# Token stores moved from ScalarE's queue to SyncE's, and extra weight for streaming heads in the pacing of attention

## The chip, the cores and the metric

The kernel runs on one core of one Trainium2 chip. The metric is the device time of an execution in microseconds (us), as the median over several executions. Six fast runs of the kernel before, on the same chip, spread by 1.0% (392.65 to 396.69 us). Runs come with a state. Only runs of the state "fast" enter a ratio; a single run of one core has the state "unknown". The granted clock is the share of its full clock that TensorE got. PSUM is where the kernel puts the products of its matmuls (pA, pV and pO in the traces), in tiles that are called banks here. Engines: PE is TensorE (PEld its weight loads), ACT is ScalarE, DVE is VectorE, POOL is GpSimd, SP is SyncE. A line of a timeline gives start and length in us, the engine and the line of the kernel, the operation, what it writes <- reads, shapes and count, and in brackets how long the engine had been idle and what ended that. The lines shown are word for word; those between them are left out.

## The reference

The program is an attention followed by a mixture of four expert networks:

```python
# attention: q, k, v of shape (4 batches, 8 heads, 768, 64)
scores = scale * q @ k.T                       # causal
# heads 0, 2, 6 ("retrieval") see every earlier key
# heads 1, 3, 4, 5, 7 ("streaming") see 4 sink keys and a window of 64
a = softmax(scores);  x = (a @ v)              # to rows: 3072 tokens x 512
# experts: E = 4, hidden 1024
p = domain_probs / domain_probs.sum(-1)
out = sum_e p[:, e] * (relu(x @ w1[e]) @ w2[e])  # 3072 x 512, float32
```

## The kernel before

The 768 positions of a batch are two chunks of 384 tokens, so attention has chunks 0 to 7. The expert networks run over 24 tiles of 128 tokens: tiles 0 to 2 together and tile 3 alone in a plain way (`plain_steps`), then ten pairs of tiles in a way with fewer products (`pair_steps`). Attention of a later chunk is put out in small steps between the matmuls of the experts; the order is fixed when the program is built.

The stores of the first four tiles, in `plain_steps`:

```python
            else:
                nc.vector.scalar_tensor_tensor(out=acc[nt], in0=ps_o, ...)   # L1002
            if e == E - 1:
                nc.scalar.dma_start(out=out[nt * P : (nt + 1) * P, :], in_=acc[nt])  # L1008
            yield FTP // 2 * mm_ns(DM), 1.4
```

The end of a streaming head (Ln and then Exp of its negative give one over the row's sum; `ps` is one of two pV banks of PSUM; `later` puts the scaling out some 1300 planned ns after this):

```python
            nc.scalar.activation(out=rc[r, :], in_=ps[o, 0:CH], func=AF.Ln, ...)   # L769
            ...
                nc.scalar.activation(out=rc[r, :], ..., func=AF.Exp, scale=-1.0)   # L779
                later(scale, g)            # L774: xT = ps * rc, which frees the bank
            ...
            yield ns + (600.0 if g == 1 else 0.0)     # planned ns of this step
```

The pacing. Each step of the experts yields its matmul time and a share; each step of attention its planned ns:

```python
    def att_ns(a):                       # planned ns of chunk a
        ns = 4000.0 if a % NCH == 0 else 6100.0
        return ns + (1100.0 + HP * 3 * 400.0 + NSH * 600.0 if a < NCH else 0.0)
    ...
    for ns, share in moe_steps():
        spent += ns * share
        while state["a"] < G and spent > plan[state["a"]][0]:
            lo, hi = plan[state["a"]]
            behind_plan = (spent - lo) / (hi - lo) * att_ns(state["a"])
            if state["steps"] is not None and state["done"] >= behind_plan:
                break
            attention_step()
```

`share` is 0.5 in the first layer of a pair, where ScalarE does the ReLUs, and 1.57 in the products of its second layer, where ScalarE has little to do: by the page of before, 94.6 us of ReLUs (L1087) against 11.2 us of copies (L1129).

The softmax here doesn't subtract the row's maximum and nothing guards it: scores larger than these inputs give would overflow.

Of the kernel before, what the change touches and what calls it, by code (L numbers as in the profile page):

```python
# [17 lines left out]
def kernel(  # L18
# [33 lines left out]
    nc = tc.nc  # L52
    P = 128
# [3 lines left out]
    NCH = S // CH  # L57
    N = B * S
    HP = H // 2
# [39 lines left out]
    def bank():  # L99
        return pA.tile([P, 512], FP32, name="pA", bufs=4)  # L100
# [4 lines left out]
    NR, NSH = len(RH), len(SH)  # L105
# [49 lines left out]
    def half(u):  # L155
        return slice(u * D, (u + 1) * D)
# [25 lines left out]
    def v_tile(b, c, h, t):  # L182

        if b:
            return v_tiles(b, c, h)[:, t, :]
        return v_tiles(b, t // TC, h)[:, t % TC, :]
# [188 lines left out]
    for h in range(H):  # L375
        if h == 2:
            nc.sync.dma_start(
                out=v_s32, in_=v[0, :, 0:NS, :].rearrange("h r d -> r h d")
# [16 lines left out]
        out=probs, in_=moe_domain_probs.rearrange("(t p) e -> p t e", p=P)  # L395
# [14 lines left out]
    def warm_up(ps, n, cols):  # L410
        for _ in range(n):
            nc.tensor.matmul(
                out=ps[:, 0:cols], lhsT=warm[:, 0:P], rhs=warm[:, 0:cols],
                start=True, stop=True,
            )
# [101 lines left out]
    def mm_ns(cols):  # L517
        return cols / 2.4 + 2.5

    def attention(b, c):  # L520
        g = b * NCH + c
# [212 lines left out]
        def values(h):  # L734
            if RETR[h]:
                yield from values_r(h)
                return
            ct, u = PLACE[h]
            if first and u == 1:
                ps = pO.tile([P, 512], FP32, name="pO", bufs=2)  # L740
            else:
                ps = pV.tile([P, 512], FP32, name="pV", bufs=2)
            if first:
                warm_up(ps, {3: 4, 4: 4, 5: 6, 7: 10}.get(h, 0), 256)
            work = []
            for es, parts in es_of[h]:
                for t, o, q0, nq in parts:
                    work.append((es, t, o, q0, nq))
            ns = 0
            for n, (es, t, o, q0, nq) in enumerate(work):  # L750
                nc.tensor.matmul(  # L751
                    out=ps[:, q0 : q0 + nq],
                    lhsT=v_tile(b, c, h, t),
                    rhs=es[:, o : o + nq],
                    start=(n == 0),
                    stop=(n == len(work) - 1),
                    skip_group_check=True,
                )
                ns += mm_ns(nq)
                if ns > 300 and n < len(work) - 1:  # L760
                    yield ns
                    ns = 0

            r, o = half(u), half(1 - u)
            pair = first and h in (3, 4)
            if not pair or u == 0:
                rc_of[0] = att.tile([P, CH], FP32, name="rc", bufs=2)
            rc = rc_of[0]
            nc.scalar.activation(  # L769
                out=rc[r, :], in_=ps[o, 0:CH], func=AF.Ln, bias=eps[o, :]  # L770
            )

            def scale(r=r, ps=ps):
                nc.vector.tensor_tensor(  # L774
                    out=xT[g][r, ct, :], in0=ps[r, 0:CH], in1=rc[r, :], op=ALU.mult
                )

            if not pair:
                nc.scalar.activation(out=rc[r, :], in_=rc[r, :], func=AF.Exp, scale=-1.0)  # L779
                later(scale, g)  # L780
            elif u == 0:
                scale_of[0] = scale
            else:
                nc.scalar.activation(out=rc, in_=rc, func=AF.Exp, scale=-1.0)
                later(scale_of[0], g)
                later(scale, g)

            yield ns + (600.0 if g == 1 else 0.0)

        def both(a, bb):  # L790

# [11 lines left out]
        if first:  # L803
# [8 lines left out]
            sink_row(5)  # L812
            sink_row(7)
            yield from both(scores(1), values(0))
            yield from transposes(2)
            yield from both(scores(3), values(2))
            x_transposes(0)
            yield from scores(4)
            yield from transposes(3)
            yield from values(1)  # L820
            yield from both(scores(5), values(3))
            yield from both(scores(6), values(4))
# [87 lines left out]
    def later(op, g):  # L910
        behind.append((clock[0] + LAG, op, g))
# [34 lines left out]
    acc = {}  # L946

    def acc_of(nt):
        n0 = 2 * FTP * CH + nt * 2 * DM if nt < 3 else 6 * KT * P - 2 * DM
        return hA[:, n0 : n0 + 2 * DM].bitcast(FP32)  # L950

    def plain_steps(nt0, tiles, e, tokens, n0):

        cols_n = tiles * P
        hs = hA[:, n0 : n0 + FTP * cols_n].rearrange("p (f x) -> p f x", f=FTP)
        require(nt0 // 3)
        x = tokens()
        ahead = 4 if nt0 == 0 and e == 0 else 1
        for f0 in [0, *range(ahead, FTP)]:
            pss = {ft: bank() for ft in range(f0, f0 + (1 if f0 else ahead))}  # L960
            cts = (0, 2, 1, 3)

            def layer1(ft, n):
                ct = cts[n]
                nc.tensor.matmul(  # L965
                    out=pss[ft][:, 0:cols_n],
                    lhsT=w1sb[:, e * DMP + ct, ft * P : (ft + 1) * P],
                    rhs=x[:, ct, :],
                    start=(n == 0),
                    stop=(n == DMP - 1),  # L970
                )

            for ft in pss:
                for n in range(DMP - 1):
                    layer1(ft, n)
            for ft, ps in pss.items():
                layer1(ft, DMP - 1)
                nc.scalar.activation(  # L978
                    out=hs[:, ft, :], in_=ps[:, 0:cols_n], func=AF.Relu
                )  # L980
                yield DMP * mm_ns(cols_n), 0.6
        for j in range(tiles):
            nt = nt0 + j
            ps_o = pO.tile([P, DM], FP32, name="pO", bufs=2)
            for ft in range(FTP):
                nc.tensor.matmul(  # L986
                    out=ps_o,
                    lhsT=hs[:, ft, j * P : (j + 1) * P],
                    rhs=w2sb[:, e * FTP + ft, :],
                    start=(ft == 0),  # L990
                    stop=(ft == FTP - 1),
                )
                if ft == FTP // 2 - 1:
                    yield FTP // 2 * mm_ns(DM), 1.4
            p_ap = p_sb[:, nt, e : e + 1]
            if e == 0:
                acc[nt] = acc_of(nt)
                nc.vector.tensor_scalar(
                    out=acc[nt], in0=ps_o, scalar1=p_ap, scalar2=None, op0=ALU.mult
                )  # L1000
            else:
                nc.vector.scalar_tensor_tensor(  # L1002
                    out=acc[nt], in0=ps_o, scalar=p_ap, in1=acc[nt],
                    op0=ALU.mult, op1=ALU.add,
                )
            if e == E - 1:

                nc.scalar.dma_start(out=out[nt * P : (nt + 1) * P, :], in_=acc[nt])  # L1008
            yield FTP // 2 * mm_ns(DM), 1.4

    PT = 2
# [207 lines left out]

    def att_ns(a):  # L1220
        ns = 4000.0 if a % NCH == 0 else 6100.0
        return ns + (1100.0 + HP * 3 * 400.0 + NSH * 600.0 if a < NCH else 0.0)

    first_pair = E * UNIT + ONE

# [26 lines left out]
    def require(a):  # L1252
        drained = False
        while state["a"] <= a:
            attention_step()
            drained = True
        if drained:
            tick(LAG)
        while any(g <= a for _, _, g in behind):
            behind.pop(0)[1]()  # L1260

    spent = 0.0
    for ns, share in moe_steps():
        spent += ns * share
        tick(ns)
# [6 lines that stand above are left out]
# [37 lines left out]
```

## Time and profile before

| | before |
|---|---|
| median of 4 runs | 396.42 us (395.07 to 397.28) |
| span of the profiled run | 392.6 us |
| TensorE busy | 376.8 us, 96% |
| longest single wait of TensorE | 3.52 us, at 76.9 us |
| late excess (after 84 us) | 4.85 us in eight places |

"Late excess" is used throughout: the distance from each matmul's start to the next, less columns / 2.4 + 2.5 ns, summed where it is over 0.15 us and the clock is full. The formula fits the trace of before: after 84 us the median distance is 56, 109, 163 and 216 ns for 128, 256, 384 and 512 columns, and the formula gives 55.8, 109.2, 162.5 and 215.8. The late excess is worked out from the starts in the trace and shows losses that busy time hides, because the ends of matmuls are modelled. The page's line on the chain that ended last says how much of the span hung on TensorE itself:

```profile
PE 75%; DMA 15%; POOL 4%; ACT 3%; issue 1%; DVE 1%; SPq 1%; ACTq 0%; POOLq 0%
```

A quarter of the chain ran through something else. The other lines of before stand in the prediction.

### The profile page before, as it was taken

To read this page: it belongs to the slowest core of one execution; us is meant where nothing else is said; L and a number is where in the kernel's file an instruction comes from. 1 tells how busy PE (TensorE), PEld (TensorE's weight loads), DVE (VectorE), ACT (ScalarE), POOL (GpSimd) and SP (SyncE) were. 2 spreads that over 40 slices of the span, in tenths; PEclk is the share of its full clock that TensorE was granted. 3 is DMA by queue.
4 is the path that set the end of the run, shared out by engine and by line. 5 is a ranking of instruction groups with operands and counts; after the bars stand their busy time and mean duration, and the time that the engine had idled before them with its cause. 6 is when DMAs were issued, how large, how long until landed. Compare 5 with 4: busy or idle time off the path is not lost.

```text
span 392.6 us, 9368 instructions
## 1 busy us (share of the span) xinstructions
PE 376.8 (96%) x3814; PEld 312.7 (80%) x3814; DVE 231.4 (59%) x516; ACT 234.4 (60%) x476; POOL 110.4 (28%) x152
## 2 busy tenths in 40 slices
PE   7989999889999997999999999999999999999996
PEld 4755456457897886889988898889988898888885
DVE  7736787516957657575654656575654556454440
ACT  3853569335767767574865667574865667450640
POOL 8834553582028206601550006601300000000000
PEclk9999999989999999999999999999999999999999
DMA  8999999999199968936890448924910210110101
GB/s 158 161 209 199 177 152 192 175 189 103 55 114 96 114 131 67 165 80 89 102 149 4 109 94 64 162 79 84 107 54 2 69 55 12 55 54 21 38 0 55
DMA packets 127192, 39.19 MB, mean 100 GB/s; under 512 B 116232, under 2 KB 120876, under 8 KB 127148
## 3 DMA queue, kind: packets, MB, share of 16 engines
q0 software_dynamic: 86816, 19.01, 56.8%
q1 hardware_dynamic: 38156, 18.13, 20.7%
q10 hardware_dynamic: 2176, 1.44, 1.4%
q8 instruction: 30, 0.49, 0.5%
q14 instruction: 14, 0.11, 0.1%
HBM read 44.88 MB, written 6.34 MB: 130 GB/s over the span
## 4 chain that ended last, share of the span: by engine, by line
PE 75%; DMA 15%; POOL 4%; ACT 3%; issue 1%; DVE 1%; SPq 1%; ACTq 0%; POOLq 0%
PE pA L1078 36%; PE pO L1111 29%; DMA w1sb<-in_moe_w_dram 5%; DMA k_rows<-in_k_dram 5%; PE pA L639 4%; DMA q<-in_q_dram 3%; PE pO L986 2%; DMA kT<-k_rows 2%; PE pA L965 2%; PE pV L687 1%; PE pV L751 1%; POOL vR L291 1%; ACT rc L769 1%; ACT es L657 1%; DVE xT L774 1%
## 5 line engine op out<-in xcount | busy, mean ns | idle before, releaser
L1078 PE MATMUL pA<-xs,w1sb 128*128 128x256 f16 x1280 | 146.4, 273 | 0.0
L1078 PEld LDWEIGHTS <-w1sb 128*128 128x128 f16 x1280 | 123.7, 98 | 14.8
L1087 ACT ACTIVATE hA<-pA 128x512 f16<-128x512 f32 x160 | 94.6, 597 | 38.6 <-PE pA L1078 36.5
L1111 PEld LDWEIGHTS <-hA 128*128 128x128 f16 x1120 | 105.3, 98 | 12.1
L657 ACT ACTIVATE es<-pA 128x384 f16<-128x384 f32 (+2 forms) x122 | 59.9, 510 | 37.8 <-PE pA L639 33.3
L1111 PE MATMUL pO<-w2sb,hA 128*128 128x256 f16 x640 | 78.1, 272 | 0.0
L293 POOL DMA_DIRECT2D vS<-in_v_dram x30 | 29.6, 986 | 140.7 <-PE pV L751 114.9
L1044 DVE TENSOR_TENSOR xs<-xT,pB 128x1024 f16<-128x1024 f16 (+1 forms) x52 | 49.5, 972 | 23.6 <-PE pA L1078 23.6
L1111 PE MATMUL pO<-tsb,hA 128*128 128x256 f16 x480 | 60.2, 272 | 0.0
L934 DVE TENSOR_TENSOR hA<-hA 128x1024 f16<-128x1024 f16 (+1 forms) x80 | 41.9, 552 | 1.1
L978 ACT ACTIVATE hA<-pA 128x384 f16<-128x384 f32 (+1 forms) x64 | 22.2, 386 | 26.1 <-PE pA L965 17.3
L965 PE MATMUL pA<-xT,w1sb 128*128 128x384 f16 (+1 forms) x256 | 31.6, 275 | 3.6 <-ACT hA L978 3.5
L986 PE MATMUL pO<-w2sb,hA 128*128 128x512 f16 x128 | 32.0, 392 | 0.5 <-DMA w2sb<-in_moe_w_dram 0.5
L965 PEld LDWEIGHTS <-w1sb 128*128 128x128 f16 x256 | 19.4, 99 | 12.1 <-issue 4.4
L661 DVE TENSOR_TENSOR es<-es,mC 128x256 f16<-128x256 f16 (+1 forms) x42 | 10.6, 255 | 29.7 <-ACT es L657 29.6
L1052 DVE TENSOR_TENSOR hA<-hA 128x512 f16<-128x512 f16 (+1 forms) x30 | 15.3, 509 | 19.6 <-ACT hA L1087 19.6
L774 DVE TENSOR_TENSOR xT<-pV,rc 64x384 f16<-64x384 f32 x37 | 20.4, 553 | 10.2 <-ACT rc L779 7.9
L661 DVE TENSOR_TENSOR es<-es,mS 128x384 f16<-128x384 f16 (+1 forms) x40 | 13.6, 345 | 20.5 <-ACT es L657 20.3
L1132 DVE TENSOR_TENSOR o<-pO,s 128x256 f32<-128x256 f32 x30 | 12.6, 421 | 20.9 <-PE pO L1111 12.6
L639 PE MATMUL pA<-qT,kR 128*128 128x384 f16 (+2 forms) x120 | 23.8, 278 | 0.8 <-ACT qT L550 0.4
L1129 ACT COPY s<-pO 128x256 f32<-128x256 f32 x30 | 11.2, 372 | 22.5 <-PE pO L1111 22.1
L769 ACT ACTIVATE rc<-pV,eps 64x384 f32<-64x384 f32 x37 | 21.3, 575 | 5.0 <-PE pV L751 4.3
(115 smaller groups left out, 335.3 us busy)
## 6 DMA issues: line engine op xcount, KB each, us to landing
pB<-p_rows SPq DMA_DIRECT2D x10, 512.0 KB, 3.7
out_dram<-o SPq DMA_DIRECT2D x19, 256.0 KB, 4.0
w1sb<-in_moe_w_dram POOLq DMA_DIRECT2D x8, 512.0 KB, 10.3
w2sb<-in_moe_w_dram POOLq DMA_DIRECT2D x4, 1024.0 KB, 13.3
vS<-in_v_dram POOLq DMA_DIRECT2D x30, 112.0 KB, 3.5
k_rows<-in_k_dram POOLq DMA_DIRECT2D x18, 128.0 KB, 4.8
q<-in_q_dram POOLq DMA_DIRECT2D x18, 128.0 KB, 6.2
vR<-in_v_dram POOLq DMA_DIRECT2D x24, 48.0 KB, 5.4
```

The lines of the kernel that those rows point to most:

```text
L293: gp.dma_start(out=t[:, :, own_v(h)], in_=windows_of(v, b, h, c))
L639: nc.tensor.matmul(out=ps[:, o : o + nq], lhsT=key_tile(b, c, h, t), rhs=qTs[b, c][:, hp, q0 : q0 + nq], start=(n == 0 or not first), stop ...
L657: nc.scalar.activation(out=es[:, 0:cols], in_=ps[:, 0:cols], func=AF.Exp, scale=SC)
L769: nc.scalar.activation(out=rc[r, :], in_=ps[o, 0:CH], func=AF.Ln, bias=eps[o, :])
L774: nc.vector.tensor_tensor(out=xT[g][r, ct, :], in0=ps[r, 0:CH], in1=rc[r, :], op=ALU.mult)
L934: nc.vector.tensor_tensor(out=out, in0=a, in1=b, op=ALU.subtract)
L965: nc.tensor.matmul(out=pss[ft][:, 0:cols_n], lhsT=w1sb[:, e * DMP + ct, ft * P : (ft + 1) * P], rhs=x[:, ct, :], start=(n == 0), stop=(n = ...
L986: nc.tensor.matmul(out=ps_o, lhsT=hs[:, ft, j * P : (j + 1) * P], rhs=w2sb[:, e * FTP + ft, :], start=(ft == 0), stop=(ft == FTP - 1),)
L1044: nc.vector.tensor_tensor(out=o, in0=xin, in1=pb.to_broadcast([P, DMP, n, P]), op=ALU.mult)
L1078: nc.tensor.matmul(out=ps[:, f * PC : (f + 1) * PC], lhsT=w1sb[:, e * DMP + ct, (f0 + f) * P : (f0 + f + 1) * P], rhs=xs[:, ct, :], start= ...
L1087: nc.scalar.activation(out=blocks[:, b0 : b0 + 2, k0 : k0 + 2, :].rearrange("p t f x -> p f t x"), in_=ps.rearrange("p (f t x) -> p f t x" ...
L1111: nc.tensor.matmul(out=ps, lhsT=a[:, k, :], rhs=b(k), start=(first and k == 0), stop=(k == KT - 1), skip_group_check=not first,)
```

## The change

It has two intents: take the stores out of the stream of an engine that computes, and spread the streaming heads, whose matmuls are few but whose work on ScalarE is not (in the trace of before, 0.34 us for the seven matmuls of a head's values product, and 0.50 + 0.575 + 0.52 = 1.6 us of ScalarE a head).

```diff
-            yield ns + (600.0 if g == 1 else 0.0)
+            yield ns + (600.0 if g == 1 else 400.0)
@@
-                nc.scalar.dma_start(out=out[nt * P : (nt + 1) * P, :], in_=acc[nt])
+                nc.sync.dma_start(out=out[nt * P : (nt + 1) * P, :], in_=acc[nt])
@@
     def att_ns(a):
         ns = 4000.0 if a % NCH == 0 else 6100.0
-        return ns + (1100.0 + HP * 3 * 400.0 + NSH * 600.0 if a < NCH else 0.0)
+        ns += NSH * (600.0 if a == 1 else 400.0)
+        return ns + (600.0 + HP * 3 * 400.0 if a < NCH else 0.0)
```

## The prediction

> **What bounds the kernel now.** I read the page first, then the waits of TensorE, the timeline where its longest wait falls, busy time by stretch, and the chain that ended last.
>
> ```profile
> span 392.6 us, 9368 instructions
> ...
> PE 376.8 (96%) x3814; PEld 312.7 (80%) x3814; DVE 231.4 (59%) x516; ACT 234.4 (60%) x476; POOL 110.4 (28%) x152
> ...
> PE   7989999889999997999999999999999999999996
> ...
> PEclk9999999989999999999999999999999999999999
> ```
>
> TensorE (PE) is busy 96% of the span; ScalarE (ACT) and VectorE (DVE) are near 60%. One digit of the granted clock is an 8, in the slice from 78.5 to 88.3 us. Busy time can hide slow matmuls, so I also took the distance from each matmul's start to the next. From 84 us to the end it is columns / 2.4 + 2.5 ns (109 ns for 256 columns) almost everywhere; the excess over that is 4.85 us, in eight places. So late in the kernel only those eight places can be won, and before them one large wait:
>
> ```profile
> PE pA L965 <- ACT hA L978: 3.5, 1, 3.5
> PE pV L751 <- DVE xT L774: 3.4, 6, 0.8
> ```
>
> (Columns: total us, times, longest.) The first, in the timeline:
>
> ```profile
> 69.46 3.90 SPq L250 DMA_TRANSPOSE kT<-k_rows  x3
> ...
> 74.05 4.83 SPq L250 DMA_TRANSPOSE qT<-q  x3
> ...
> 74.73 5.29 ACTq L1008 DMA_DIRECT2D out_dram<-hA  x3
> ...
> 75.82 1.06 PE L965 MATMUL pA<-xT,w1sb 128*128 128x128 f16 x16
> ...
> 80.06 1.57 ACT L978 ACTIVATE hA<-pA 128x128 f16<-128x128 f32 x7 [7.87 <-DMA kT<-k_rows]
> 80.39 1.35 PE L965 MATMUL pA<-xT,w1sb 128*128 128x128 f16 x16 [3.52 <-ACT hA L978]
> ```
>
> The three stores of token tiles 0 to 2 (L1008) stand in ScalarE's own stream. They issue at 74.73, 78.79 and 79.68. Ahead of the second and third stands a wait on a semaphore that ended when the second and third kT transposes of SyncE's queue landed; the store then signals that same semaphore. So the two hardware queues share a few completion semaphores in turn, and ScalarE waited for a transfer that its store has nothing to do with. Behind the stores stand the ReLUs of tile 3; TensorE filled its four PSUM banks (16 matmuls) and stood for 3.52 us. What followed is in the stretches (PE, PEld, DVE, ACT, POOL busy, clock, DMA):
>
> ```profile
> 78.00:80.00 2.00, 0.00 (x0) 0.00 (x0) 0.79 (x2) 0.00 (x0) 1.76 (x3) 1.00 2.12 171
> 80.00:82.00 2.00, 1.61 (x18) 1.33 (x18) 0.00 (x0) 1.74 (x8) 1.86 (x6) 0.75 1.31 159
> 82.00:84.00 2.00, 2.00 (x6) 0.73 (x5) 0.00 (x0) 0.06 (x1) 1.59 (x4) 0.50 1.89 147
> 84.00:86.00 2.00, 2.00 (x27) 1.56 (x26) 1.11 (x2) 0.89 (x4) 1.41 (x2) 0.90 1.35 301
> ```
>
> After the wait the clock is halved: 2 us x (0.25 + 0.50 + 0.10) = 1.7 us lost. The second kind of wait is in the chain:
>
> ```profile
> 149.52 0.50 ACT es L657
> 150.04 0.36 DVE es L661
> 150.40 0.47 DVE xT L774
> ...
> 153.14 0.57 DVE xT L774
> 153.75 0.34 PE pV L751 x7
> ```
>
> A streaming head's values product (L751) needs one of two pV banks; a bank is free when ScalarE has done the head's Ln and Exp (L769, L779) and VectorE the scaling (L774). The chain runs through them at the end of attention chunks 2, 3, 5 and 7.
>
> [...] one stretch of 3.41 us at 0.5, after the only wait of that length. [...] ReLUs whose inputs were ready near 76 us start at 80.06, behind the stores. [...] the trace has 575 (Ln) and about 520 (Exp).
>
> **The change, part by part.** *Stores.* Four stores of 256 KB leave ScalarE's stream (4 x 0.35 us of issue) and join SyncE's. In emission order the first three now stand behind the six transposes of chunk 2, which have issued by 78.9 us, so they leave near 79 to 80 us or a little later if they wait for a semaphore. They read the accumulators in hA; the first ReLU that overwrites those (pair 0, fifth block of w1) runs about 2 us into pair 0, near 93 us in the new time, so it should not wait. The ReLUs of tile 3 start near 76 us and TensorE runs on, as it does for later experts of tile 3 (1.79 + 1.73 us each without a break). Gain: 3.5 us of wait, and the 1.7 us of half clock. [...] the timed runs need not all have paid the whole; I count 1.2. Sum 4.7.
>
> *Pacing.* The pacing hands out attention steps in proportion to planned ns. From the yields, even chunks hold 3790 (plan 4000), odd ones 6059 (plan 6100); a streaming head is 177.5 for scores and 177.5 for values. Each values step now adds 400, and the plan 5 x 400 = 2000, so a chunk still fits its stretch, but after each streaming head more matmuls of the experts come before the next. A pair is 128 x 109.2 + 112 x 109.2 ns = 26.2 us; half a product is 873 ns of it, weighted by 1.57.
>
> Chunk 3 has 0.93 pairs = 24.4 us: 6100 / 24.4 us x 1.57 x 873 ns = 343 planned ns per half product, so a head (355) every 1.0 halves. Now 8100 gives 456, a head of 755 every 1.66. Chunk 2 (24.5 us): 1.58 to 2.25. Chunks 5 and 7 (1.45 pairs): 1.61 to 2.59. Chunks 4 and 6 (1.55 pairs): 2.63 to 3.7. ScalarE needs 0.50 + 0.575 + 0.52 = 1.6 us a head. In chunk 3 a head came every 0.87 + 0.36 = 1.23 us, too fast; it will be 1.45 + 0.36 = 1.81 us.
>
> The measured excess sorts by this spacing: chunk 3 (1.0 halves) 0.95 + 0.90 + 0.62 = 2.47 us; chunk 2 (1.58) 0.91; chunks 5 and 7 (1.61) 0.23 + 0.51 each; chunks 4 and 6 (2.63) none. Read off at the new spacings: chunk 3 keeps about 0.8, chunk 2 about 0.2, the rest nothing. Gain 4.85 - 1.0 = 3.8 us. Matmuls and ACTIVATEs stay the same in number.
>
> *Chunk 1.* It keeps 600 per head; its plan falls from 15000 to 14500 against 14376 of work, so its steps come up to 0.8 us (3.3% of 24.4 us) later. They end well before tile 3 needs them: no gain, no loss. In chunk 0 the added 400 only moves the deferred-scaling clock, and I see no reordering.
>
> *What it can cost.* Chunk 2's retrieval heads come earlier: planned work when tile 3 is nearly done rises by 6000 / 4000, and the whole stage starts some 5 us earlier. Its first scores then stand near 86.6 us, and the qT transposes landed at about 86.1 (the next q load waited for them until 86.10). The copies of keys into windows (2.4 us of VectorE) fall just before pair 0's second expert, whose scaled input (0.97 us, L1044) they delay. I allow 0.3 us each.
>
> Sum: 4.7 + 3.8 - 0.6 = 7.9 us; 396.43 - 7.9 = 388.5 us.
>
> **The rivals.** (a) *The wait only moves.* [...] the stores could hold up the sink rows or the next transposes, and ScalarE's first ReLU of pair 0 could wait for a store to land. For: SyncE's transposes wait for semaphores in the same way, and DMA is dense until 92 us. Against: between 90 and 104 us SyncE waits for x_one anyway, and nothing that TensorE needs soon stands behind the stores. It would leave about 2 us of the stores' gain: 391. (b) *Attention becomes bound by DMA or VectorE.* With 5 us gone, transfers that were just hidden show. For: the 0.5 us of slack at qT. Against: all loads of chunk 3 are issued by 91 us and used after 110. It would cost 1 to 3 us: 390 to 391. (c) *The pacing shifts the jam onto retrieval heads.* They get squeezed: an odd-chunk retrieval head (1261 planned ns) took 1261 / 343 = 3.7 halves in chunk 3 and takes 2.8. ScalarE needs 4 x 0.6 = 2.4 us for it, and 2.8 halves with their own matmuls are 3.7 us, so it fits. If it didn't, the pacing part would gain 1 to 2 us: 391. (d) *Everything goes*, clock loss in each run included: 5.2 + 4.85 = 10 us: 386.4.
>
> **Range and chances.** The stall and the eight places are measured, so a total under 4 us needs two rivals at once. Most of the doubt is the half clock (0 to 1.7 us), what chunk 3 keeps, and the new waits of chunk 2. Range 385.8 to 391.5 us. Faster by 2% means under 388.5, just my estimate, so it is even: faster 0.49, within 2% 0.49, slower 0.02.
>
> **What would show it.** Right, if the new trace has no wait of TensorE near 77 us, ReLUs of tile 3 starting near 76, a granted clock of 1.0 from 6 us on, three stores on SyncE's queue behind the qT transposes, pair 0 starting near 91 instead of 95.9 us, and the wait for xT (3.4 us) below 1. Wrong, if ScalarE again waits for a transfer before tile 3 or pair 0, if TensorE waits for qT near 87 us or for xs near 95, or if waits for es of retrieval heads appear in chunks 2 to 7.

## The result, and the profile after

| | before | changed |
|---|---|---|
| median of 4 runs | 396.42 us | 385.77 us (384.33 to 386.57) |
| span of the profiled run | 392.6 us | 382.6 us |
| late excess | 4.85 us | 0.46 us in two places |

The ratio is 0.973 (95% interval 0.969 to 0.977), so it is faster by 2.7%. A ratio here is the mean time of one kernel's fast runs over that of the other's fast runs of the same rounds, so it is not quite the ratio of the medians. The gain of 10.65 us between the medians is more than the 7.9 predicted, and 385.77 lies just under the predicted range.

The page of the changed kernel (instruction busy times, then the slices and the chain):

```profile
PE 374.2 (98%) x3814; PEld 312.2 (82%) x3814; DVE 235.5 (62%) x516; ACT 233.6 (61%) x476; POOL 111.7 (29%) x152
...
PE   8989999999999999999999999999999999999996
...
PEclk9999999999999999999999999999999999999999
...
PE 86%; DMA 7%; POOL 3%; DVE 2%; ACT 1%; issue 0%; POOLq 0%; ACTq 0%
```

TensorE's time and the counts are as before; the dents in its row after the first slices are gone, and so is the 8 in the clock. More of the chain is TensorE itself (86% for 75%). The waits of TensorE (total us, times, longest), the three longest:

```profile
PE pO L412 <- DVE early L397: 1.3, 1, 1.3
PE pO L751 <- DMA vS<-in_v_dram: 1.2, 1, 1.2
PE pV L687 <- ACT es L657: 0.9, 2, 0.8
```

Both waits of before, for the ReLUs (3.5 us) and for xT (3.4 us), are gone. What is left are waits of the first 20 us and of the first chunks. The timeline where the large wait was:

```profile
74.39 4.61 SPq L250 DMA_TRANSPOSE qT<-q  x3
75.77 1.95 PE L965 MATMUL pA<-xT,w1sb 128*128 128x128 f16 x32
76.20 1.84 ACT L978 ACTIVATE hA<-pA 128x128 f16<-128x128 f32 x8 [3.42 <-PE pA L965]
77.56 1.89 PE L986 MATMUL pO<-w2sb,hA 128*128 128x512 f16 x8
79.09 12.98 SPq L1007 DMA_DIRECT2D out_dram<-hA  x4
```

The ReLUs of tile 3 start at 76.20 in place of 80.06 (0.43 us after their first matmul in place of 4.24), and TensorE goes from w1 to w2 without a break. The stores now stand in SyncE's stream behind the transposes: the first issues at 79.09, the fourth ends at 92.07. TensorE does not wait for them.

The two places of late excess left are 0.19 us at 87.4 us, in tile 3, and 0.27 us at 94.8 us, where the scaled input of pair 0's second expert is late:

```profile
L1077 PEld LDWEIGHTS <-w1sb 128*128 128x128 f16 x1280 | 122.5, 98 | 14.4 <-DVE xs L1043 0.4
```

### The profile page after: what moved, and what is told of

Its sections match the earlier page's. It is cut to its first block, busy times and chain, and to the rows that moved or that the text cites.

```text
span 382.6 us, 9369 instructions
## 1 busy us (share of the span) xinstructions
PE 374.2 (98%) x3814; PEld 312.2 (82%) x3814; DVE 235.5 (62%) x516; ACT 233.6 (61%) x476; POOL 111.7 (29%) x152
## 4 chain that ended last, share of the span: by engine, by line
PE 86%; DMA 7%; POOL 3%; DVE 2%; ACT 1%; issue 0%; POOLq 0%; ACTq 0%
PE pA L1077 36%; PE pO L1110 32%; DMA w2sb<-in_moe_w_dram 7%; PE pO L986 5%; PE pA L639 5%; PE pA L965 4%; PE pV L687 2%; PE pV L751 2%; POOL vS L297 1%; ACT es L657 1%; POOL vR L291 1%; DVE kS L277 0%; POOL early L436 0%; DVE hA L1002 0%; POOL w1sb L322 0%
## 5 line engine op out<-in xcount | busy, mean ns | idle before, releaser
L1077 PE MATMUL pA<-xs,w1sb 128*128 128x256 f16 x1280 | 148.1, 272 | 0.1
L1110 PEld LDWEIGHTS <-hA 128*128 128x128 f16 x1120 | 106.6, 98 | 12.9
L1110 PE MATMUL pO<-tsb,hA 128*128 128x256 f16 x480 | 58.6, 272 | 0.0
L934 DVE TENSOR_TENSOR hA<-hA 128x1024 f16<-128x1024 f16 (+1 forms) x80 | 42.0, 553 | 1.1
L986 PE MATMUL pO<-w2sb,hA 128*128 128x512 f16 x128 | 30.5, 379 | 0.3 <-DMA w2sb<-in_moe_w_dram 0.3
L986 PEld LDWEIGHTS <-hA 128*128 128x128 f16 x128 | 11.9, 98 | 12.2 <-issue 0.5
L291 POOL DMA_DIRECT2D vR<-in_v_dram x24 | 19.0, 811 | 5.5 <-DMA w2sb<-in_moe_w_dram 4.0
```

What stands on the lines that cost most here:

```text
L291: gp.dma_start(out=t[:, :, 0:D], in_=rows_of(v, b, h, c))
L934: nc.vector.tensor_tensor(out=out, in0=a, in1=b, op=ALU.subtract)
L986: nc.tensor.matmul(out=ps_o, lhsT=hs[:, ft, j * P : (j + 1) * P], rhs=w2sb[:, e * FTP + ft, :], start=(ft == 0), stop=(ft == FTP - 1),)
L1077: nc.tensor.matmul(out=ps[:, f * PC : (f + 1) * PC], lhsT=w1sb[:, e * DMP + ct, (f0 + f) * P : (f0 + f + 1) * P], rhs=xs[:, ct, :], start= ...
L1110: nc.tensor.matmul(out=ps, lhsT=a[:, k, :], rhs=b(k), start=(first and k == 0), stop=(k == KT - 1), skip_group_check=not first,)
```

## The experiments

Twelve runs were made in three sets, each set on a chip of its own. All gave correct results. The runs of before differ from chip to chip (medians over all runs, slow ones too, 395.33, 395.74 and 393.36 us), so each time is read against the runs of before of its own set, or against kernels of the same set.

### Set 1: the two parts alone, and what makes a streaming head late

**e1_stores_only**: only the stores move.

```diff
-                nc.scalar.dma_start(out=out[nt * P : (nt + 1) * P, :], in_=acc[nt])
+                nc.sync.dma_start(out=out[nt * P : (nt + 1) * P, :], in_=acc[nt])
```

> Only the stores move to SyncE; the pacing is that of before. Theory A (the two parts are separate losses and add up): no wait of TensorE near 77 us, no half clock there, and the late excess of 4.85 us stays within 0.5 us of that at the ends of chunks 2, 3, 5 and 7; span about 5.2 us under before (3.5 of wait, 1.7 of half clock), a little under if the timed runs of before did not all pay the half clock: 4.5 to 5.5 us faster, about 391.5. Theory B (the pacing does most, the stall only moves): under 3 us faster, with a new wait of ScalarE or TensorE before pair 0.

Measured: 388.97 us (388.82 to 389.80), ratio 0.986 (0.980 to 0.993), that is some 5.5 us. The span of the profiled run is 387.1 us. The wait near 77 us and the half clock after it are gone (granted clock 0.999 for 0.994), and the late excess is 4.85 us as before, at the same heads:

```profile
PE pV L751 <- DVE xT L774: 3.4, 6, 0.8
```

So this part gains the wait and the half clock, and nothing of the gain comes back as a new wait. Theory A holds for it. One thing was not expected: the four runs spread by 1.0 us, while the six fast runs of before beside them spread by 4.0 us (392.65 to 396.69).

**e2_pacing_only**: the changed kernel with `nc.scalar` put back in the stores.

> Only the pacing changes; the four stores stay on ScalarE. Theory A (separate losses): the wait of 3.5 us near 77 us and the half clock stay, the eight late places are gone; 4.3 to 5.0 us faster than before, about 391.7. Theory B (the parts depend on each other: the later steps of chunk 1 or the earlier heads of chunk 2 change the stall): the stall near 77 us differs from 3.5 us by over 1 us, and the gain is not the difference between the changed kernel and the stores alone.

Measured: 391.87 us (391.25 to 392.72), ratio 0.993 (0.988 to 0.998), that is some 2.8 us, where 4.3 to 5.0 was expected. The late excess fell to 0.46 us, as in the changed kernel, so the heads were cured. But the wait near 77 us grew:

```profile
69.11 1.18 SPq L713 DMA_TRANSPOSE xT<-x_pair  x1
70.46 0.46 SPq L1027 DMA_DIRECT2D pB<-p_rows  x1
70.98 4.29 SPq L250 DMA_TRANSPOSE kT<-k_rows  x3
75.33 6.93 ACTq L1007 DMA_DIRECT2D out_dram<-hA  x3
...
82.64 1.65 PE L965 MATMUL pA<-xT,w1sb 128*128 128x128 f16 x14 [4.84 <-ACT hA L978]
```

Before, the x_pair transpose issued at 66.02 and the first kT transpose at 69.46. Here they come 3.1 and 1.5 us later, and the three stores hold ScalarE for 6.93 us in place of 5.29. The second and third store again wait for the semaphores that two kT transposes signal (until 79.85 and 81.88). The parts are thus not independent; theory B's second form was right about that. Set 3 asks why.

**e4_sums_later**: stores on SyncE, pacing of before, and each half of the fourth sum is put out half a product later, so that the scaling of a head comes before it on VectorE.

```diff
-        fourth_sum(0)
-        yield half
+        yield half
+        fourth_sum(0)
```

(and the same for `fourth_sum(1)`)

> Stores on SyncE, pacing of before, and each half of the fourth sum (0.68 us of VectorE, which waits for a product of TensorE) is put out one half product later. Theory P (a head needs 1.6 us of ScalarE, and heads that come every 1.2 us jam there): the late excess stays at 4 us or more, the time is that of the stores alone. Theory V (ScalarE is done in time, but the scaling that frees the pV bank stands on VectorE behind a fourth sum that waits for TensorE): the late excess falls under 2 us, so some 3 us faster than the stores alone, with no change of pacing at all.

Measured: 388.56 us (388.35 to 388.85), 0.4 us under the stores alone. The late excess is 4.5 us: chunk 2 fell from 0.91 to 0.30, chunk 3 rose from 2.47 to 2.77, chunks 5 and 7 stayed. Theory V in this form, a fourth sum ahead of the scaling, holds for one place of the eight. The excess stayed over 4 us, as theory P named it, but that does not show ScalarE to be the limit at the rest: other work than a fourth sum can stand ahead of the scaling on VectorE (see below).

**e3_half_pacing**: 200 planned ns for 400.

```diff
-            yield ns + (600.0 if g == 1 else 400.0)
+            yield ns + (600.0 if g == 1 else 200.0)
@@
-        ns += NSH * (600.0 if a == 1 else 400.0)
+        ns += NSH * (600.0 if a == 1 else 200.0)
```

> The changed kernel with 200 in place of 400 planned ns per streaming head, in the step and in the plan (chunks 2 to 7). A head then comes every 1.39 half products in chunk 3, 1.98 in chunk 2 and 2.17 in chunks 5 and 7 (between before and changed). Reading the excess off against the spacing as the prediction did: 1.4 us in chunk 3, 0.4 in chunk 2, 0.2 in each of 5 and 7, so 2 to 2.4 us of late excess and about that much slower than the changed kernel. Rival (a threshold: what counts is whether the scaling is handed out before or behind a fourth sum, which comes in whole steps): the excess is either near none or near that of before in each chunk, not in between.

Measured: 385.01 us (384.79 to 386.36), ratio 0.976 (0.971 to 0.982). The late excess over 0.15 us is 0.66 us in one place of chunk 3 and 0.19 us in tile 3; chunks 2, 5 and 7 have none. That is far under the 2 to 2.4 us that the prediction's way of reading gave. What is left is one wait:

```profile
144.99 0.34 PE L751 MATMUL pV<-es,vS 128*128 128x48 f16 x7 [0.50 <-DVE xT L774]
```

The rival's "near none or near that of before" is right for chunks 2, 5 and 7, but chunk 3 lies in between.

### What decides whether a head waits

The traces of set 1, of before and of the changed kernel show two things that differ. Two pV banks mean that the values product of one head can start once the head two before it has been scaled. So take, for each streaming head, the time from the end of the values product two heads before to its own start, and take its excess off: that is the other work that TensorE had to do in between. The last column is how long after the end of its Exp the scaling of the head two before began, the scaling that frees the bank.

| where | work between (us) | excess (us) | scaling begins after Exp (us) |
|---|---|---|---|
| before, chunk 2 | 3.16, 2.98, 2.83 | 0, 0.91, 0.05 | 0.82, 1.42, 0.67 |
| before, chunk 3 | 2.29, 3.06, 1.95 | 0.95, 0.90, 0.62 | 0.82, 1.10, 0.03 |
| before, chunk 5 (7 is alike) | 3.16, 2.33, 2.43 | 0.23, 0.51, 0.05 | 1.16, 0.82, 0.33 |
| half pacing, chunk 3 | 3.16, 2.18, 2.58 | 0.08, 0.66, 0.05 | 0.82, 0.82, 0.33 |
| changed, chunk 3 | 3.16, 2.98, 2.80 | 0, 0, 0 | 0.03, 0.03, 0.03 |

The work between does not decide alone: with 2.98 us of it, chunk 2 of before lost 0.91 us and chunk 3 of the changed kernel nothing.

The wait ends when a turnover ends: Ln, Exp and scaling, with what stands ahead of them. The turnover in the waits, the sum of work and excess, is 2.5 to 3.4 us, and 3.9 to 4.0 us in the two worst (2.98 + 0.91 and 3.06 + 0.90), so it is no fixed number. Where heads crowd, Ln and Exp queue behind one another and behind the exp of scores. In the trace of before, at chunk 3:

```profile
148.36 0.58 ACT L769 ACTIVATE rc<-pV,eps 64x384 f32<-64x384 f32 x1
148.82 0.34 PE L751 MATMUL pV<-es,vS 128*128 128x48 f16 x7
148.97 0.52 ACT L779 ACTIVATE rc<-rc 64x384 f32<-64x384 f32 x1
150.03 0.58 ACT L769 ACTIVATE rc<-pV,eps 64x384 f32<-64x384 f32 x1
150.64 0.52 ACT L779 ACTIVATE rc<-rc 64x384 f32<-64x384 f32 x1
151.46 0.50 ACT L657 ACTIVATE es<-pA 128x384 f16<-128x384 f32 x1
151.99 0.36 DVE L661 TENSOR_TENSOR es<-es,mS 128x384 f16<-128x384 f16 x1 [0.53 <-ACT es L657]
152.26 0.54 DVE L774 TENSOR_TENSOR xT<-pV,rc 64x384 f16<-64x384 f32 x1
152.95 0.34 PE L751 MATMUL pV<-es,vS 128*128 128x48 f16 x7 [0.73 <-DVE xT L774]
```

The values product of 148.82 is done at 149.16; its Ln starts at 150.03, after the Exp of the head before and the scores' exp of another (0.50 us from 149.52, in the chain that the prediction shows). Its Exp ends at 151.16, yet its scaling begins only at 152.26: it stands on VectorE behind the mask product of another head (L661), which waits for ScalarE's exp of that head's scores. At seven of the eight places of before the scaling stands so, 0.82 to 1.42 us after its Exp (three times with a sum or an addition, L934 or L1132, standing between as well). In the changed kernel, at the same chunk:

```profile
142.41 0.34 PE L751 MATMUL pV<-es,vS 128*128 128x48 f16 x7
142.56 0.55 DVE L774 TENSOR_TENSOR xT<-pV,rc 64x384 f16<-64x384 f32 x1 [0.80 <-ACT rc L779]
143.12 0.57 ACT L769 ACTIVATE rc<-pV,eps 64x384 f32<-64x384 f32 x1
```

Here Ln starts 0.37 us after its product has ended (142.75 to 143.12). The smallest work between two streaming heads is 2.80 us, and no head waits. The scaling at 142.56 follows its Exp at once (L779, by the bracket), and so do, within 0.2 us, 28 of the 30 of chunks 2 to 7. The waits of VectorE say the same: the scaling waited for nothing later than its Exp 13 times in before (first line, total us, times, longest) and 30 times in the changed kernel:

```profile
DVE xT L774 <- ACT rc L779: 9.3, 13, 2.3
...
DVE xT L774 <- ACT rc L779: 25.2, 30, 1.4
```

So the weight of 400 did two things. It put more work between the heads, and it moved the scaling ahead of a mask product on VectorE. As the code reads, `later` lets 1300 planned ns pass, of attention and of the experts: a values step of before and a half product are 177.5 + 873 = 1050, so the next steps of attention, with their mask, can come first; with 400 more they are 1450. An estimate from these numbers: taking at each of the eight places the smaller of excess and delay, the delay accounts for up to 4.1 of the 4.85 us. No run moved the scaling alone (1300 made smaller, the pacing of before), so how much of the gain each of the two made is not shown.

### Set 2: is it the wait or the issue, how far can pacing go, and the spread

**e5_scalar_later**: the kernel before, but the three stores stay on ScalarE and come 7 us later.

```diff
-            if e == E - 1:
+            if e == E - 1 and nt == 3:
                 nc.scalar.dma_start(out=out[nt * P : (nt + 1) * P, :], in_=acc[nt])
@@  before tile 3's steps of expert e
+            if e == 2:
+                for nt in range(3):
+                    nc.scalar.dma_start(out=out[nt * P : (nt + 1) * P, :], in_=acc[nt])
```

> Kernel before, but the three stores of tiles 0 to 2 stay on ScalarE's queue and are put out 7 us later, ahead of tile 3's third expert; by then (about 83 us) the transposes whose semaphores they take have landed. Theory A (ScalarE lost its time to a wait for an unrelated transfer on a shared completion semaphore): no wait of over 0.5 us near 77 us, three issues of 0.35 us each, time within 0.7 us of the run with the stores on SyncE (about 389 us). Theory Q (stores on ScalarE's queue cost it the time themselves): ScalarE still stands for several us at the stores and TensorE with it, 393 us or more.

Measured: 388.89 us (388.33 to 390.13), ratio 0.984 (0.980 to 0.988), as fast as the stores on SyncE. The trace:

```profile
76.33 1.84 ACT L978 ACTIVATE hA<-pA 128x128 f16<-128x128 f32 x8 [4.04 <-PE pA L965]
...
81.46 1.35 ACTq L1190 DMA_DIRECT2D out_dram<-hA  x3
```

Three stores, 1.35 us in a piece, no wait of TensorE. Theory A holds and theory Q falls. ScalarE's queue did not cost the time by itself; the moment did, at which the semaphores were still taken by transposes in flight: in the trace of before, where the second and third waited for such a semaphore, the three took 5.29 us.

**e6_double_pacing**: 800 planned ns for 400, in the step and in the plan.

> The changed kernel with 800 in place of 400 planned ns per streaming head. Theory T (a threshold: TensorE needs 2.8 us of other work between the values of one head and of the head after next, and 400 already gives that): no excess at streaming heads, and retrieval heads, which now come a quarter faster than in the changed kernel, start to wait for es or for a score bank if anything does; same time as the changed kernel within 0.5 us if they don't, 1 to 2 us slower if they do. Theory I (the excess falls steadily with spacing): nothing left to win, also the same time. A wait for es of L687 late in the kernel tells that the pacing has been taken too far.

Measured: 386.27 us (385.73 to 386.64), against 385.59 for the changed kernel in the same set (below); the intervals of the two ratios overlap widely. No streaming head waits; waits of retrieval heads for es grow:

```profile
PE pV L687 <- ACT es L657: 1.3, 3, 0.8
```

The late excess is 1.6 us in six places, the largest 0.55 us at a retrieval head at 124.0 us, which waits for es (0.38 us by the view). The other two waits of the line stand in the changed kernel too (0.9, 2, 0.8). So the trace shows what overdone pacing begins to cost, 1.1 us more of late excess than at 400; the times do not tell the two apart.

**b1_before_again** and **a1_changed_again**: both kernels once more.

> The kernel before once more, for its spread. The timed runs of before spread by 4 us with granted clocks of 1.00, 0.995 and 0.990, while the kernel with only the stores moved spreads by 1 us at 0.996 to 1.00. Theory A: the wait near 77 us ends when a DMA lands, so its length differs from run to run (3 to 6 us), and one or two half clock windows of 3.4 us follow it: 1.7 or 3.4 us. Rival: the spread comes from the first 20 us, with a half clock there.

> The changed kernel on the same chip as its variants: 384 to 386 us; spans 382.6 to 383.5 where the clock is 1.0, no excess over 0.4 us after 84 us. If three of four runs again show a granted clock of 0.994, the half window comes from the first 20 us, where TensorE still waits for 1 to 2 us at a time.

Measured: before 393.91 us in its one run (span 392.2 us), with a wait of 3.17 us near 77 us and one stretch at half clock, of 3.41 us from 80.54 us (in the trace of before: 3.41 us from 80.99). The changed kernel 385.59 us (384.89 to 386.47), ratio 0.975 (0.971 to 0.979), with a clock of 1.0 in three runs of four and 0.999 in the other. Its late excess is again 0.19 + 0.27 us. Of the fast runs of before in this set, three have a clock of 0.995 to 0.996 (393.8, 392.3 and 393.4 us of span) and three 0.990 to 0.991 (395.8, 395.4, 394.0). One such stretch takes 3.41 / 2 = 1.7 of 392 us, 0.004, so as an estimate from these clocks the former lost about one and the latter about two, and the end of the span a little (in the trace of before the clock is a half from 391.6 us on).

Where the second can come from, the trace of the double pacing shows (busy PE, PEld, DVE, ACT, POOL, clock, DMA):

```profile
18.00:20.00 2.00, 1.17 (x13) 0.84 (x13) 1.69 (x5) 1.13 (x4) 0.57 (x1) 1.00 1.51 185
20.00:22.00 2.00, 0.88 (x8) 0.88 (x9) 0.11 (x1) 0.18 (x1) 1.24 (x3) 0.68 1.28 204
22.00:24.00 2.00, 2.00 (x11) 1.41 (x10) 1.12 (x2) 0.91 (x2) 0.72 (x1) 0.50 1.24 207
```

After waits of 0.93 and 1.64 us (by the starts of the matmuls) at 17.5 and 19.4 us, which every kernel here has in some length (by the view 0.83 and 1.26 us in before, 0.76 and 1.21 us in the changed kernel), the clock fell to a half from 20.7 to 24.1 us. That is chunk 0, where the order of TensorE's work is the same before and after the change. The trace of e9 (below) has such a stretch at half clock too, from 21.6 to 25.0 us. The length of these waits alone does not tell when it comes: by the view they are 0.76 and 1.48 us here, and 0.93 and 1.90 us in the second trace of the changed kernel, which kept the full clock. So the rival for the spread is right in part: the traces of e6 and e9 lose such a stretch there (3.4 us each), and both traces of before lose one after the wait at 77 us (3.41 us each). That the runs of before with 0.990 lost both was not seen in a trace.

### Set 3: why pacing alone gained less than expected

**e8_pacing_old_chunk1**: pacing alone, and chunk 1 keeps its plan.

```diff
-        return ns + (600.0 + HP * 3 * 400.0 if a < NCH else 0.0)
+        return ns + (1100.0 + HP * 3 * 400.0 if a < NCH else 0.0)
```

> Pacing alone, stores on ScalarE, and chunk 1's plan left at the 15000 ns of before; the order of VectorE's instructions up to chunk 2 is then that of before. Theory C (the lower plan of chunk 1 put out its last retrieval head later, so SyncE's transposes of chunk 2 came 1.5 us later and the stores that wait for them on ScalarE too: 5.0 us of wait in the pacing-only trace against 3.3 to 3.7 in the two traces of before): first kT transpose near 69.5 us again, wait of 3.2 to 3.8 us, some 1.3 us faster than pacing alone with the new plan, about 390.5. Rival (DMA timing differs from run to run by that much): the wait is 4.5 us or more here too, or pacing alone with the new plan shows under 4 us in its second trace.

Measured: 390.23 us (389.78 to 392.87), ratio 0.993 (0.988 to 0.998). The trace:

```profile
66.16 1.32 SPq L713 DMA_TRANSPOSE xT<-x_pair  x1
67.65 0.46 SPq L1027 DMA_DIRECT2D pB<-p_rows  x1
69.93 3.91 SPq L250 DMA_TRANSPOSE kT<-k_rows  x3
...
80.44 1.39 PE L965 MATMUL pA<-xT,w1sb 128*128 128x128 f16 x16 [3.43 <-ACT hA L978]
```

**p2_pacing_again**: pacing alone with the new plan, as in set 1.

> Pacing alone as in the changed kernel, a second trace of it: theory C expects the x_pair transpose of chunk 1 near 69 us, the first kT transpose near 71 us and a wait of 4.5 to 5.3 us near 77 us; the rival expects a wait anywhere from 3 to 5.

Measured: 390.77 us in one run, span 389.1 us. The x_pair transpose issues at 68.59, the first kT transpose at 70.94, and TensorE waits 4.42 us. With the old plan of chunk 1 these were 66.16, 69.93 and 3.43, and the profiled span was 388.1 us.

So theory C fits: with chunk 1's plan lowered from 15000 to 14500, its last retrieval head is put out later, its x_pair transpose stands ahead of the six transposes of chunk 2 in SyncE's stream, and the stores on ScalarE wait for those. Three traces with the old plan and stores on ScalarE waited 3.52, 3.17 and 3.43 us, two with the new plan 4.84 and 4.42. It is worth about 1 us, and only as long as the stores stand on ScalarE. The wait with the new plan came out a little under the 4.5 us that theory C named. The profiled spans of this set, 388.1 and 389.1 us, are 1.0 us apart where 1.3 was named; the ratios of e2 and e8, of different sets, don't tell the two apart.

**e7_chunk1_plan**: the changed kernel with chunk 1's plan back at 15000 (the same edit as above).

> The changed kernel with chunk 1's plan back at 15000 ns. With the stores on SyncE nothing that TensorE needs stands behind those transposes, so theory C expects no change in time (within 0.5 us of the changed kernel, 385 to 386 us); the first kT transpose is near 69.5 to 70 us again. If the lower plan of chunk 1 had a gain of its own, this is 1 us or more slower.

Measured: 384.68 us (384.48 to 385.84), ratio 0.978 (0.974 to 0.982) on a chip on which before is faster too. The late excess is 0.18 + 0.33 us, as in the changed kernel. In this set there was no run of the changed kernel itself; its two medians on other chips are 385.77 and 385.59. So the new plan of chunk 1 has no gain that shows.

**e9_chunk2_half**: as e7, with 200 planned ns in chunk 2 alone.

```diff
-            yield ns + (600.0 if g == 1 else 400.0)
+            yield ns + (600.0 if g == 1 else 200.0 if g == 2 else 400.0)
```

(and the same in `att_ns`)

> As the run before, with 200 planned ns per streaming head in chunk 2 alone. The half-paced run showed no excess in chunk 2, and none of the 0.27 us that the changed kernel loses before pair 0's second expert. So 0.3 us better than the run before at best, under what these rounds can tell; the trace shows whether the 0.27 us is gone and no new place has come.

Measured: 384.92 us (384.37 to 385.39), the same as e7. The 0.27 us before pair 0's second expert is gone, as expected, but a new place of 0.35 us has come at 116.9 us, at a score product of a retrieval head. There is nothing to win here that these rounds could show, and no version ran that clearly beats the changed kernel.

## Why the prediction was wrong

The direction and the mechanism of the stores held, and the waits of the streaming heads went, as forecast. The odds for over 2% were even, so that it came says little. The time fell 0.03 us under the range. What failed are sizes in its sum, and for the streaming heads also a part of the mechanism. The two profiled runs show each term:

| term | predicted gain | traces |
|---|---|---|
| wait near 77 us | 3.5 us | 3.7 us |
| half clock after it | 1.2 us | 1.7 us |
| late excess of before | 3.8 us | 4.85 us |
| new waits | -0.6 us | -0.46 us |
| sum | 7.9 us | 9.8 us; spans differ by 10.0 us |

(3.7 us is the excess between the starts of the two matmuls around the wait, in place of the wait that the view gives. That the new waits came out near the 0.6 allowed is in part luck: one of the two allowances was not needed, and 0.19 us of the 0.46, in tile 3, was not foreseen.)

**The step that failed.** It is "Read off at the new spacings: chunk 3 keeps about 0.8, chunk 2 about 0.2, the rest nothing". It took the excess as falling steadily with the average spacing of heads, with ScalarE's 1.6 us a head as what is short. Both chunks kept nothing. The half-paced run shows it most plainly: the same reading gave 2 to 2.4 us for it, and it had 0.66 us in chunk 3 and none in the other chunks. Chunk 5 of before and chunk 3 of the changed kernel have nearly the same average spacing (1.61 and 1.66 half products), yet the former loses up to 0.51 us at a head and the latter nothing. What the traces show in place of an average is a turnover of the bank, head by head, against the work between: 2.5 to 3.8 us from the end of the product to the end of its scaling at the eight places of before, of which at seven places 0.82 to 1.42 us is the scaling standing on VectorE behind another head's mask product; in chunk 3 of the changed kernel it is 1.9 to 2.6 us, against 2.80 us of work or more. The prediction saw that the added 400 moves the clock of the deferred scaling, but for chunk 0 only; it moves it in chunks 2 to 7 as well. How much came from the spacing and how much from this order stays open. This step is 1.05 us of the 1.9 us by which the traces beat the sum.

**The half clock.** The prediction counted 1.2 of 1.7 us, since its author estimated that the timed runs need not all have paid the whole. All five traces with stores on ScalarE at the old place (two of before, three of pacing alone) show the half clock after it (granted clock of the span 0.994 to 0.996). Timed runs of before with a granted clock of 1.0 exist too (one in set 1, one in set 3), so a discount is right in kind, but it was not due between the two profiled runs: 0.5 us. The rest of the miss, 10.65 us between the medians against 10.0 between the profiled spans, lies in the runs: the timed runs of before were up to 3.0 us over its profiled run (394.26 us), and those of the changed kernel up to 2.2 us over its own (384.33 us). That a longer wait near 77 us in other runs of before makes this up is likely, as its end hangs on when a transfer lands, but it was not traced.

**What held.** The stores stand behind the qT transposes at 79.09 us, the ReLUs start at 76.20 us, pair 0 starts at 90.92 us (predicted near 91), and no wait came back at the stores: rival (a) did not happen. The first scores of chunk 2 ran at 86.54 us with no wait for qT, so that allowance was not needed. The scaled input of pair 0's second expert was late by 0.27 us at 94.8 us, where 0.3 us was allowed; that is one of the prediction's own signs of being wrong ("for xs near 95"), at a size that it had counted. Rival (b) took the form of this one place. Rival (c), retrieval heads squeezed, did not happen at 400 and began at 800, with 0.55 us at one head. Rival (d), everything goes, at 386.4 us, was the nearest to what came.

**Chunk 1.** "No gain, no loss" is right for the changed kernel, as e7 shows. It was not right for the pacing alone, where the later steps lengthened the stores' wait by about 1 us. The prediction named steps up to 0.8 us later; in set 3 the x_pair transpose came 2.4 us later (68.59 in place of 66.16 us). The prediction did not look at the two parts apart, where this would have shown.

## What to carry to other kernels

A DMA issue in the stream of a computing engine cost far more than its 0.35 us here (three took 5.29 us, and 1.35 us where the other queue's transfers had landed): look for what it waits on, not only for its data but for a completion semaphore that another queue's transfer still holds, and either issue it from a queue that computes nothing or after that transfer has landed. Where a buffer's turnover sets the pace, compare the turnover with the work between each pair of uses, one by one: an average spacing hides the pair that waits. Take the turnover apart too: here up to 1.42 us of it was a finished Exp whose scaling stood behind other work on VectorE, and a planned time that was meant to set the spacing also set that order. And when two parts of a change touch the same queue, look at each of them alone before adding their gains.

## What the runs show of the hardware

- Two issues waited for another engine's transfers. In the trace of before SyncE's DMAs signal eight completion semaphores (numbers 100, 102 and 104 to 109), and all eight DMAs that ScalarE issues signal one of these (each but 109). The second store waited for number 105 until 78.71 us, when SyncE's second kT transpose landed, and the third for number 106 until 79.60 us, when the third landed; they issued at 78.79 and 79.68 us and signal the same two numbers. The issues themselves took 0.34 to 0.37 us each, yet the move of the stores to SyncE gained about 5.5 us (e1_stores_only).
- The clock fell to a half after waits of TensorE: in the trace of before for 3.41 us from 80.99 us, after a wait of 3.52 us; in the second trace of before for 3.41 us from 80.54 us, after one of 3.17 us (3.33 us by the starts of the matmuls); in the trace of e6 for 3.4 us from 20.7 us, after waits of 0.93 and 1.64 us that were broken by matmuls. In the second trace of the changed kernel waits of 0.93 and 1.90 us were followed by the full clock. How long TensorE must wait before the clock falls, no run here finds.
- The ReLUs of tile 3 did not pass the stores ahead of them in ScalarE's stream: their first matmul started at 75.82 us in before, and they started at 80.06 us, 0.38 us after the third store issued. With the stores out of the way they started 0.43 us after their first matmul. An Ln of 384 columns took 575 ns in these traces and an Exp of 384 about 520.
